# A new order table for a hand-scheduled attention and feed-forward kernel: the operations behind the first 86 in another order, and some of them on other engines

## Chip, cores and metric

One Trainium2 chip, one of its NeuronCores. The metric is the device time of the program in microseconds, the median of several runs; smaller is better. A profile is one further execution, taken by the hardware profiler, with its own time.

## The reference

```python
B, H, S, D = 4, 8, 768, 64           # batch, heads, sequence, head size
scores = q @ k.transpose(0, 1, 3, 2) / sqrt(D)
keep = (pos_k < 4) | ((pos_q - pos_k >= 0) & (pos_q - pos_k < 128))
a = softmax(where(keep, scores, -1e9))
x = (a @ v).transpose(0, 2, 1, 3).reshape(B * S, H * D)      # 3072 x 512
h = maximum(x @ w_in, 0)                                      # w_in 512 x 2048
out = (h * h) @ w_out                                         # w_out 2048 x 512
```

Attention with 4 sink keys and a window of 128 keys, then a two-layer network with a squared ReLU. All inputs and the output are float32; inside, the matmuls run on bfloat16.

## The kernel before

**Tiles.** The four batches are worked through one after the other, each batch in three blocks of 256 query rows (s = 0, 1, 2). A block's attention handles head pairs; pairs 0 and 1, and 2 and 3, are taken together. TensorE makes transposed scores of a head pair in a PSUM bank `ps` (L614, function `scores`); ScalarE takes the exponential into the SBUF tile `expm` (L635, `expo`); the window's triangles are cut out either by a multiplication with `tri` on VectorE (L647) or by two selects on GpSimd (L219, `domask`); TensorE multiplies with the values into `po` (L683, `values`); VectorE divides by the sums into `xn_sb` (L699, L700, `norm`). Sink keys and values go through a small product `pk` (L573) and `es`. The result has to be transposed for the network: batches 0 and 1 do it on TensorE (`px`, L732, "bridge") with a copy to `xT`; batches 2 and 3 do it by DMA transposes from SyncE's queue (L714).

**Loads.** In batch 0 and 1, q and k are cast by DMAs that GpSimd issues (L373) and transposed on TensorE (`pt`, L508), then copied to `qkT` ("unload", by VectorE or ScalarE). In batches 2 and 3, GpSimd issues the casting loads of q, k and v (L404, L416), and SyncE issues DMA transposes into `qkT` (L462). w_in and w_out come by four loads each, also from GpSimd (L317 for w_out).

**Network.** Batch 0's first layer is done plainly (L764), that of the others in a form with seven products per quad and sums of inputs and weights (L892; sums `xs`, `wi`). The second layer of two row blocks is seven products (L1239) with sums `sg` and `wt`; a quarter of the result is copied out of PSUM to the buffer `osb` and others are added to it (L1253). The store of a pair of row blocks is one DMA from SyncE (L1282). `osb` has two buffers, so a third pair waits for the first one's store to land.

**Order.** 996 operations are created by the code above; each has a number (in order of creation), the engines that it may run on, and the buffers that it takes. The table `ORDER` is a string of these numbers. `Plan.run` goes through it and records each operation's instructions; so the table sets the order of instructions on every engine and every queue. A letter behind a number (p, d, a, g) chooses the engine (TensorE, VectorE, ScalarE, GpSimd); without it the first of its list is taken. `+0` or `+1` chooses the PSUM pool. Engines run their own instructions in that order, and wait by semaphores for what they need. DMAs stand in the instruction order of the engine that issues them, so one that must wait holds up what is behind it on that engine.

**Numbers used below.** 156, 162, 168, 174: first layer of batch 0, block 0 (L764). 81: its sink scores. 106, 108, 116, 118: masks of batch 0, block 1, for head pairs 0, 1, 2, 3. 109, 111, 119, 121: the values of these pairs. 123, 125: the block's two bridge transposes; 31, 32: the last V loads of batch 0; 33 to 36: the loads of w_out; 208: sink values of batch 1; 129: an unload of batch 0, block 2; 137: the scores that read it; 172: a relu. 466 to 477: the DMA transposes of batch 2's q and k; 692 to 709: the loads of batch 3. 296, 315, 334: the three stores of batch 0; 548, 586, 567: the stores of batch 1. 553, 556: first and second product of a chain of the second layer; 555: the copy between them into `osb`.

Of the kernel before, what the change touches and what calls it, by code (L numbers as in the profile page):

```python
# [20 lines left out]
ORDER = """  # L21
994 0 1 2 7 8 9 10 11 12 13 14 15 16 17 18 995+0 3 5 19 20 21 6 79 22 23 24 25 55d 56d 57+0 58 59 60a 83+0 85 103+1
105 26 27 28 62d 61d 63+1 64 67d 68d 65a 69+0 70 71 72 66a 84+1 73a 74a 75+1 76 78 91+0 86 77a 93 80 113+1 87+0 92+1
89 94 95+0 97 115 88 90 96 98 114+1 99+0 101 117 100 104+0 102 4 29 106 30 107 81+1 31 82 156+0 109+1 116 118 162+0
108d 32 111 157 112 119+1 168+0 121 120 110 123+1 122 125 174+1 163 126 335 169 124a 171+0 131+0 128+1 33 208 34 164
133 170a 175 35 36 37 172 38 132 39 40 158 130a 129a 144+1 146 137+0 176 136+0 147d 145+1 138 140 139d 177+0 278 134+0
148 159+1 135 149d 141d 142+0 279 143 173a 41 178 150+1 282+0 42 151 179a 152+0 43 153a 280 160 154 44 165+0 155a 45
274 189+1 166 180+1 275 276 284 161a 127 285 190d 277 281 283 181 337 286 287 46 192+1 289 196+0 193 200+0 194 197
167a 47 195a 201 297 336 288 48 202 338 183+0 198a 199a 203a 212+0+0 49 290 182 292 184d 215 294 230+0+1 291 299 50
293 298 191 213 231 186+1 204+0 233 295 185 187d 51 52 300 206a 301+0 251+1 303 248+0 205 188a 207a 232d 249a 304 253  # L30
252a 339 316 305d 296 302 219+1+0 216 317 308 53 318 209 306 307d 220 54 222 214 210+0 250a 319 309 234 448 237+0+1
310 311 211 235+0 238 217+0 240 218 236 223 340 466 239d 320+0 449 312 241d 221 450 322 256+0+0 451 259 257 313 452
453 323 454 455 314 341 321 456 242+0 244+0 457 324 458 224+1 327 459 325 460 461 243 471 225 326 226+0 254+1 246 245a
329 228 330 229a 247a 227 331 315 347+1 343 363+1 342 349 469 345 328 332 365 348 364 344 346 255 351 350 333 367
263+1+1 462 366 353 369d 352 479 354 260d 264 368 370 355d 379+0 470 467 266 358 356 468 395+0 258 359 463 371 372
357a 374 360d 361 381 265 373a 380 376 267d 375 474 383 261+0 382 362a 377 397 396 268+0 477 384 262 385 399 386 270+0
475 398 269 387d 272 273 378a 400 473 401 464 478 465 402 271a 489+0+0 390 411 492 490 388 392 403d 391 334 406 404
407 482+0+0 412 393 432+0 483 433 389 476 434 416+1 472 413 394 408 409 436 414 405 417 418 435 534+0 410a 438 420 692
419 536 437 530 422 439 415 421 693 423 532 440 537 485 443 441 491 424 694 427 533 538 444 695 442a 429 696 697 493
531 445 425 539 494+0 428 446 426a 535 495 480+0 540 430 698 447a 498+1+0 481 699 484 486 544 700 499 543 487+0 549  # L40
501 431 488 568 545 713 572+0 505+0+0 569 574 500d 546 541 508 506 542 573 521+0+0 547 710 714 701 579 522 570 575 576
514+1+0 509d 571 496 702 577 703 524 715 578 507 510+0 548 515 523d 582 580 550 723 497 581 583 502 517 585 553+0 551
503+0 511 704 711 516 554 584 587 588 592+0 589 504 594 525 526+0 705 590 518d 555 527 593 717 556 557 591 519+0 712
716 596 520 558 559d 598 552 749+0+0 706 707 595 722 560 561 563 512 750 752 597 599 513 600 562 742+0+0 753d 565d 528
564 603 743 601 751 602 566 604 745 586 726+0+0 529 720 605d 721 608+0 727 609 606 610 660+1 661 662 611 729 624 644+0
718 663 626 612 730 719 724+0 613 625 567 614 725 615 754+0 616 607 728 664 665 645 617 666 646 755 667 618a 648 647
668 619 744 620 649 627 650d 651 731+0 746 669 621 671 672 708 622 676+0 670a 677 673 732 652 674 747+0 623 678 655
653 679 680 656 681 675a 748 657 658 628+1 629 682 630 659 733+1+0 683 774 632 631 734 778+0 684 654a 775 634 685 735
633 779 635 686a 780 636 776 687 688 736 777 709 756 781 689d 690 758+0+1 759 637 782 761 639 640 638a 737 738+0 783
641d 739 642 691a 785 765+0+0 762d 784 760 643 797+0 768 766 793 787 757 799 794 788 769 789 763+0 795 740 767d 790d  # L50
741 791 764 798 786 831 800 801 836+1 837 834 802 832 792 838d 852+0 833 854d 853 840 804 796 855 856 803 839 806 858d
770+0 771 807 857 812 835 813 859 842 808 841 843 772 805 814 810 816+1 860 773 863 861 817 865 844d 864 847 845 809
823 866 818d 846a 868 848 867a 872+0 869 849 874 871 920+0 862 819 850 820 922 873 904+1 870 815 921 905 875 906d 876
877 923 851a 924 821 936 822d 878 879 907 925 811 926 908 880 825 883 827 937 927 881 826 938 882 828 910 885 824 829
884 909 886 888+1 911 928d 889 887 940+0 890 892 942 891 929 893 939 931 894d 932 912 915 930a 895 933 896 934 943 913
916 897 899 914a 944 900 945 935 917 830 946 901 898 941 959+0 902 918 949 947 919a 903 955 957 950 951 956 953 948
961 960 974 962 966 952d 976 978+1 963 975 958 979 964 981+1 965d 954 980 968 967 977 982 983d 970 969 985 984 986 989
972 987 971 988 990 973 993 992 991
"""
DUMMIES = {  # L60
    995: 29, 58: 8, 63: 10, 64: 4, 83: 3, 91: 3, 97: 3,
# [1345 lines left out]
```

## Time and profile before

| | |
|---|---|
| time, median of 3 runs | 210.18 us (210.08 to 210.21) |
| profiled execution, own time | 209.92 us |
| its span, first to last instruction | 208.1 us |
| TensorE busy | 198.7 us, 95% |
| VectorE, ScalarE, GpSimd busy | 175.4, 140.0, 94.0 us |
| granted TensorE clock | 1.000 |

Engines are named PE (TensorE matmuls), PEld (its weight loads), DVE (VectorE), ACT (ScalarE), POOL (GpSimd) and SP (SyncE); a q behind the name is the engine's queue, which issues DMAs. A row of a timeline reads: start, length, engine and line, operation, what it writes from what it reads, count; in brackets the idle time before it and who ended it. A row of waits reads: who waited for whom, total, times, longest. The ends of matmuls are modelled, and successive matmuls overlap, so a row of sixteen ends later than the next one begins.

### The profile page before, as it was taken

What the parts mean: (1) busy time and instruction counts of PE and PEld (TensorE: products, weight loads), DVE (VectorE), ACT (ScalarE), POOL (GpSimd) and SP (SyncE); (2) the same over time, 40 slices, a digit from 0 to 9 for tenths busy, and PEclk for the clock granted to TensorE, in tenths of its full rate; (3) what the DMA queues carried; (4) which work ended last, traced back from release to release, by engine and by line L of the source; (5) the groups of instructions that cost most, each with busy time, mean ns of one, the idle gap of its engine ahead of it and who ended that gap; (6) DMA issues with size and microseconds to landing.
All of it is one profiled execution on the core that took longest, in us unless ns stands there. A gap on an engine that the chain in (4) does not pass through costs nothing.

```text
span 208.1 us, 6073 instructions
## 1 busy us (share of the span) xinstructions
PE 198.7 (95%) x2524; PEld 178.7 (86%) x2524; DVE 175.4 (84%) x343; ACT 140.0 (67%) x218; POOL 94.0 (45%) x134
## 2 busy tenths in 40 slices
PE   7779989999999999999999999999999999999993
PEld 7548878998888889889878989998889999999892
DVE  5844647988998899999997988999999998999753
ACT  2686679865895579999977459789892176475010
POOL 7999983597289907319629937100230000000000
PEclk9999999999999999999999999999999999999999
DMA  5999999999999999999999998902022230110205
GB/s 169 278 187 206 174 197 215 166 150 142 158 68 146 147 198 154 166 142 82 143 133 214 110 149 161 186 3 50 3 50 104 30 126 3 41 60 3 101 3 202
DMA packets 93995, 26.12 MB, mean 125 GB/s; under 512 B 86800, under 2 KB 91408, under 8 KB 93968
## 3 DMA queue, kind: packets, MB, share of 16 engines
q0 software_dynamic: 69248, 12.59, 87.1%
q1 hardware_dynamic: 24536, 13.01, 28.7%
q8 instruction: 20, 0.33, 0.6%
q10 hardware_dynamic: 184, 0.14, 0.2%
q14 instruction: 7, 0.06, 0.1%
HBM read 27.30 MB, written 6.29 MB: 161 GB/s over the span
## 4 chain that ended last, share of the span: by engine, by line
PE 70%; DMA 13%; POOL 5%; ACT 4%; DVE 3%; SPq 2%; issue 1%; ACTq 0%; DVEq 0%; POOLq 0%
PE py L1239 31%; PE pm L892 23%; DMA w_out_sb<-in_moe_w_out_dram 6%; PE po L683 5%; PE ps L614 5%; DMA qn<-in_q_dram 4%; DMA qr<-in_q_dram 3%; PE pm L764 2%; POOL expm L219 2%; PE py L1100 2%; SPq L352 2%; ACT expm L635 1%; PE pt L508 1%; ACT gT_sb L915 1%; POOL qn L373 1%
## 5 line engine op out<-in xcount | busy, mean ns | idle before, releaser
L635 ACT ACTIVATE expm<-ps 128x1024 bf16<-128x1024 f32 (+1 forms) x48 | 43.8, 956 | 4.3 <-PE ps L614 3.9
L219 POOL TENSOR_SCALAR_AFFINE_SELECT expm<-expm 128x512 bf16<-128x512 bf16 x30 | 20.9, 726 | 42.2 <-ACT expm L635 33.6
L942 DVE CUSTOM_DVE_ANT_0 r<-pm,t 128x512 bf16<-128x512 f32 x54 | 36.1, 684 | 2.3 <-ACT t L193 1.4
L1239 PEld LDWEIGHTS <-gT_sb 128*128 128x128 bf16 x352 | 33.0, 98 | 4.6 <-issue 1.1
L892 PEld LDWEIGHTS <-w_in_sb 128*128 128x128 bf16 x384 | 32.7, 114 | 1.0 <-issue 0.5
L193 ACT ACTIVATE t<-pm 128x512 f32<-128x512 f32 x42 | 24.9, 599 | 12.3 <-PE pm L892 11.1
L193 ACT ACTIVATE osb<-py 128x256 f32<-128x256 f32 x36 | 13.6, 384 | 26.1 <-PE py L1239 23.7
L1239 PEld LDWEIGHTS <-sg 128*128 128x128 bf16 x264 | 24.9, 98 | 3.4 <-issue 0.8
L892 PEld LDWEIGHTS <-wi 128*128 128x128 bf16 x288 | 24.8, 114 | 0.8 <-issue 0.5
L1239 PE MATMUL py<-wt,sg 128*128 128x256 bf16 x176 | 22.8, 273 | 0.0
L1239 PE MATMUL py<-w_out_sb,gT_sb 128*128 128x256 bf16 x176 | 22.7, 273 | 0.0
L1239 PE MATMUL py<-wt,gT_sb 128*128 128x256 bf16 x176 | 22.7, 273 | 0.0
L764 PE MATMUL pm<-xT,w_in_sb 128*128 128x256 bf16 x192 | 22.5, 273 | 0.1
L915 ACT ACTIVATE gT_sb<-r 128x1024 bf16<-128x1024 bf16 x21 | 22.1, 1058 | 0.7 <-DVE r L942 0.7
L892 PE MATMUL pm<-xs,w_in_sb 128*128 128x256 bf16 (+1 forms) x192 | 21.3, 246 | 0.0
L892 PE MATMUL pm<-xs,wi 128*128 128x256 bf16 (+1 forms) x192 | 21.2, 246 | 0.0
L764 PEld LDWEIGHTS <-w_in_sb 128*128 128x128 bf16 x192 | 20.6, 114 | 0.6 <-issue 0.2
L683 PE MATMUL po<-v,expm 128*128 128x65 bf16 x352 | 18.0, 193 | 0.4 <-ACT expm L635 0.3
L700 DVE TENSOR_TENSOR xn_sb<-po,rc 128x512 bf16<-128x512 f32 (+1 forms) x28 | 17.2, 615 | 1.0
L683 PEld LDWEIGHTS <-expm 128*128 128x128 bf16 x352 | 16.8, 97 | 1.4 <-issue 0.6
L614 PE MATMUL ps<-qkT 64*128 64x128 bf16 (+1 forms) x256 | 14.5, 238 | 1.4 <-ACT qkT L193 1.1
L1253 DVE TENSOR_TENSOR osb<-py,osb 128x256 f32<-128x256 f32 x33 | 13.3, 418 | 2.8 <-PE py L1239 1.9
(107 smaller groups left out, 372.1 us busy)
## 6 DMA issues: line engine op xcount, KB each, us to landing
out_dram<-osb SPq DMA_DIRECT2D x11, 512.0 KB, 3.1
v<-in_v_dram POOLq DMA_DIRECT2D x24, 128.0 KB, 7.0
qn<-in_k_dram POOLq DMA_DIRECT2D x20, 128.0 KB, 6.6
qn<-in_q_dram POOLq DMA_DIRECT2D x20, 128.0 KB, 6.9
w_in_sb<-in_moe_w_in_dram POOLq DMA_DIRECT2D x4, 512.0 KB, 10.1
w_out_sb<-in_moe_w_out_dram POOLq DMA_DIRECT2D x4, 512.0 KB, 9.8
qr<-in_k_dram SPq DMA_DIRECT2D x4, 256.0 KB, 5.3
qr<-in_q_dram SPq DMA_DIRECT2D x4, 256.0 KB, 4.8
```

Source lines behind the costliest of these rows:

```text
L193: return nc.scalar.activation(out=dst, in_=src, func=AF.Copy)
L219: nc.gpsimd.affine_select(out=e_tile, in_=e_tile, compare_op=ALU.is_ge, fill=fill, base=i - 1, pattern=[[0, n], [1 if i else -1, 128]], ch ...
L614: nc.tensor.matmul(ps[:, h2, o:o + w], lhsT=qkT_sb[r, m, 1, c, :], rhs=qkT_sb[r, m, 0, qb:qb + w // 128, :], start=(i == 0 and not biased) ...
L635: nc.scalar.activation(out=x[:, :, o:512], in_=bank_t["s", b, s, m][:, :, o:512], func=AF.Exp, scale=scale)
L683: touch(("po", b, s, m0), e, nc.tensor.matmul(pv[:, i, h2, :], lhsT=lhsT, rhs=rhs, start=(n_ == 0), stop=(n_ == len(mms) - 1)), j)
L700: touch(("po", b, s, m0), e, nc.vector.tensor_tensor(out=xn_sb[:, 2 * s:2 * s + 2, 128 * (m0 + j0):128 * (m0 + j0 + nj)].rearrange("p i (j ...
L764: nc.tensor.matmul(pm[:, i, :], lhsT=w_in_sb[:, fb // 4, kb, fb % 4:512:4], rhs=xT[:, c0 // 256:(c0 + cw) // 256, kb, :], start=(kb == 0), ...
L892: touch(tag, e, nc.tensor.matmul(y[:, bk, i, :], lhsT=weights(name, f0 + i, a), rhs=rhs[:, a, :], start=fresh and i == 0 and a == 0, stop= ...
L915: nc.scalar.activation(out=d, in_=x, func=AF.Square)
L942: touch(tag, e, nc.vector._custom_dve(TENSOR_ADD_SAT, out=d.rearrange("p n c -> p (n c)"), in0=T["y"][:, 1].rearrange("p n c -> p (n c)"), ...
L1239: touch((b, u), e, nc.tensor.matmul(region(name), lhsT=x[:, i, :], rhs=w_[:, i, :], start=first and i == 0, stop=i == HB - 1, skip_group_c ...
L1253: ins = nc.vector.tensor_tensor(out=d, in0=region(of), in1=d, op=ALU.add)
```

## The change

The string `ORDER` is replaced. The first 86 words stay; behind them the same operations stand in another order, some with another engine letter or another PSUM pool. Nothing else in the file differs.

In all, 31 operations go from ScalarE to VectorE, 22 from VectorE to ScalarE, 6 masks from VectorE to GpSimd, and 6 masks and one building of sink values from GpSimd to VectorE. The order of the DMAs changes too: on SyncE, the third store of batch 0 (334) goes from behind ten of the twelve DMA transposes of batch 2 to behind three of them, and the first store of batch 1 (548) from behind five of the next transposes to behind seven.

The diff, cut:

```diff
@@ -21,41 +21,41 @@
 105 26 27 28 62d 61d 63+1 64 67d 68d 65a 69+0 70 71 72 66a 84+1 73a 74a 75+1 76 78 91+0 86 77a 93 80 113+1 87+0 92+1
-89 94 95+0 97 115 88 90 96 98 114+1 99+0 101 117 100 104+0 102 4 29 106 30 107 81+1 31 82 156+0 109+1 116 118 162+0
-108d 32 111 157 112 119+1 168+0 121 120 110 123+1 122 125 174+1 163 126 335 169 124a 171+0 131+0 128+1 33 208 34 164
-133 170a 175 35 36 37 172 38 132 39 40 158 130a 129a 144+1 146 137+0 176 136+0 147d 145+1 138 140 139d 177+0 278 134+0
...
-310 311 211 235+0 238 217+0 240 218 236 223 340 466 239d 320+0 449 312 241d 221 450 322 256+0+0 451 259 257 313 452
...
+89 94 95+0 97 115 88 90 96 98 114+1 99+0 101 117 100 104+0 102 4 29 106 156+1 30 81+0 157d 107 116 118 82 31 162+1
+119+1 109+0 163 110 120 108 158a 121 32 127 33 111 34 168+0 35 112 123+1 122 125 169 164a 174+1 126 124 208d 171+0 36
+131+1 170a 175 335 133 128+0 172 129 132 176 278 37 144+1 280 38 137+0 130a 136+0 146 177+0 39 140 145+1 40 41 42 43
...
+345 347+1 254+1 331 344 255 349 363+1 466 456 348 333 457 351 458 350 365 364 332 328 367 334 469 470 353 459 263+1+1
...
+716 575 524 715 576 525d 514+1+0 515 702 509 522 548 523 577 714 571 579 578 581 587 703 580 553+0 502d 550 582 704
+584 555 583 510+0 588 517 556 503+0 585 705 511 589 706 518d 554 557d 526+0 591 504 712 592+0 516 717 519+0 558 594
...
```

More of the change, by code (lines that the diff above doesn't have):

```diff
@@ L23 @@
 105 26 27 28 62d 61d 63+1 64 67d 68d 65a 69+0 70 71 72 66a 84+1 73a 74a 75+1 76 78 91+0 86 77a 93 80 113+1 87+0 92+1
-89 94 95+0 97 115 88 90 96 98 114+1 99+0 101 117 100 104+0 102 4 29 106 30 107 81+1 31 82 156+0 109+1 116 118 162+0
-108d 32 111 157 112 119+1 168+0 121 120 110 123+1 122 125 174+1 163 126 335 169 124a 171+0 131+0 128+1 33 208 34 164
-133 170a 175 35 36 37 172 38 132 39 40 158 130a 129a 144+1 146 137+0 176 136+0 147d 145+1 138 140 139d 177+0 278 134+0
-148 159+1 135 149d 141d 142+0 279 143 173a 41 178 150+1 282+0 42 151 179a 152+0 43 153a 280 160 154 44 165+0 155a 45
@@ L28 @@
[L28 to L31, printed above, removed]
-310 311 211 235+0 238 217+0 240 218 236 223 340 466 239d 320+0 449 312 241d 221 450 322 256+0+0 451 259 257 313 452
@@ L33 @@
[L33 to L57, printed above, removed]
@@ L58 @@
-972 987 971 988 990 973 993 992 991
+89 94 95+0 97 115 88 90 96 98 114+1 99+0 101 117 100 104+0 102 4 29 106 156+1 30 81+0 157d 107 116 118 82 31 162+1
+119+1 109+0 163 110 120 108 158a 121 32 127 33 111 34 168+0 35 112 123+1 122 125 169 164a 174+1 126 124 208d 171+0 36
+131+1 170a 175 335 133 128+0 172 129 132 176 278 37 144+1 280 38 137+0 130a 136+0 146 177+0 39 140 145+1 40 41 42 43
+44 45 147d 138 134+0 139d 159+1 141d 148 337 135 178 142+1 149d 150+0 143 160 151 282+0 152+0 173a 284d 46 336 153 154
@@ new lines @@
+274 279 275 276 179a 165+1 281 155a 161 166 180+1 47 167a 338 189+0 48 283 277 196+0 285 289 181 190 200+0 286d 49 339
+192+1 287 50 288 193 290 51 202a 197 201 195a 198a 297 194 203a 292 52 183+0 191a 199 299 212+0+0 291 213 294d 184d
+293 295 215 230+0+1 204+1 186+1 231 205 182 233 298 53 301+0 248+0 216 296 185 234d 187 188 206 207a 316 303 251+0 304
+232d 250a 341 249a 305 54 219+0+1 252a 302 300 306 308 209 220 210+0 318 253 222 211 223 237+0+1 221 307 240 235+0 448
+309 311 214 238 320+0 449 217+0 450 310 236 342 467 322d 312 451 323 313 452 239d 453 218 324 256+0+0 257 314 454 317
@@ new lines @@
+224+1 325 241d 455 321 259 225 319 315 468 226+0 227a 242+1 243 340 244+0 228 326 327 245 330 229a 329 246 247a 343
+345 347+1 254+1 331 344 255 349 363+1 466 456 348 333 457 351 458 350 365 364 332 328 367 334 469 470 353 459 263+1+1
+460 366 352 258 354 346 266 368 369d 260 370 471 461 355d 264 358 356 371 462 360d 379+0 395+0 357a 381 359 380 374
+372 397d 463 361 373a 362a 375 376 396 261+0 383 377 265 398 464 465 267 399 382 474 385 268+0 262 269 384 386 378a
+270+0 272 401 476 387d 475 400 273 402 478 271a 388 489+0+0 411 403d 390 404 492 473 391 406 490 414 392 412 407
@@ new lines @@
+482+0+0 393 413 432+0 692 389 483 693 434 433 416+1 436 417 472 408 418 405 477 409 493 435 410a 534+0 394 419 438 420
+422 437 530 439 694 695 713 421 423 440 536 424 443 415 532 445 441 537 696 697 444 425 427 428 698 491 538 711 485
+426a 531 533 494+0 535 699 446 479 539 429 495 442a 430 540d 480+0 484 481 486 498+1+0 499 431a 501 544 447 487+0
+572+0 543 488 710 545 568 700 701 574 505+0+0 547 541 508 569 573 570 542 546d 506 549 496 551 500d 497 521+0+0 507d
+716 575 524 715 576 525d 514+1+0 515 702 509 522 548 523 577 714 571 579 578 581 587 703 580 553+0 502d 550 582 704
@@ new lines @@
+584 555 583 510+0 588 517 556 503+0 585 705 511 589 706 518d 554 557d 526+0 591 504 712 592+0 516 717 519+0 558 594
+593 520 527 596 590 749+0+0 595 512 598 559d 552 752 513 560 750 597 562 599 742+0+0 753d 743 563 600d 745 561 564
+751d 603 565 726+0+0 727 528 601 722 529 566 602 604 608+0 609 660+1 723 605d 707 720 661 610 606 721 624 718 611 662
+729 612 719 613 663 614 724+0 725 607 644+0 730 615 625 744 626 754+0 728 755 746 616 664 619 666 645 665 617 646 627
+667 618a 567 620 668 647 648 731+0 621d 669 671 649 672 650 622 651 670a 676+0 673 732 652 678 674 623 675a 747+0 677
@@ new lines @@
+655 628+1 653 748 680 679 657 656 629 630 682 681 658 733+1+0 774 734 683 775 776 684 685 632 659 778+0 779 736 687
+686a 586 631 688 689d 634 690 654a 633 635 758+0+1 780d 781 735 636 759 756 639 637 782 737 738+0 641d 761 739 640 740
+741 642 638a 777 783 784 785 691a 643 793 765+0+0 787 794 795 788 768 766 708 762d 797+0 789 790d 799 798 760 709 786
+831 804 800 832 757 791 836+1 763+0 812 852+0 801 838 833 796 837 834 802 767 764 769d 853 792 805 854 856 855 839 840
+842 858 835 803d 857 770+0 813 841 771 843 807 844d 806 859 847 845 860 816+1 863 848 808 861 814 809d 772 864 818
@@ new lines @@
+849d 850 773 810 851a 819 820d 904+1 865 868 866 920+0 846a 867a 821 872+0 874 869 870 873 815 811 862 822d 936 921
+817 922 823 876 875 825 923 878 877 938 826 824 879 828d 827 880d 871 924 925 883 926 885 881 884 829 888+1 939 905
+906 886 890d 889 908 927 882 907 892 928d 887a 910 940+0 891 909 937 894 911 893 929 895 931 912 932 930 942 913 896
+933d 897 943 914a 941 898 934 899 944 915 830 935 916 901 917 900 945 959+0 946 950 918 902 919a 949 903 955 952 961
+974 947 957 951 958 956 978+1 948 962 963 976 953 975 977 960 964 954 966 979 965 981+0 968 969 967 980 983 984 970
@@ L59 @@
+982 985 986 989 971d 972 973 987 988 990 993 992 991
 """
```

## Prediction, made before the changed kernel ran

> **What bounds the kernel now.** I read the page first, then who TensorE waited for, then the order of time on GpSimd, TensorE and the queue of SyncE.
>
> ```profile
> span 208.1 us, 6073 instructions
> ...
> PE 198.7 (95%) x2524; PEld 178.7 (86%) x2524; DVE 175.4 (84%) x343; ACT 140.0 (67%) x218; POOL 94.0 (45%) x134
> ```
>
> TensorE is busy for 95% of the span. The change removes and adds no instruction, so TensorE's own work stays; only its waits can go or come. The first 86 operations stand as they did; on TensorE they reach to 16.8 us, so I asked for its waits from 15 us to the last matmul:
>
> ```profile
> PE ps L614 <- ACT qkT L193: 0.6, 1, 0.6
> PE px L732 <- DVE xn_sb L700: 0.4, 1, 0.4
> PE po L683 <- ACT expm L635: 0.3, 1, 0.3
> PE ps L614 <- ACT r L776: 0.3, 1, 0.3
> PE pt L508 <- DMA qn<-in_q_dram: 0.2, 1, 0.2
> PE pk L573 <- ACT expm L635: 0.2, 1, 0.2
> ```
>
> The columns are total, times and longest. The sum is 2.0 us, and the third row (at 15.07 us) belongs to operation 97, which is in the unchanged part. So 1.7 us, 0.8% of the span, is all that a better order can take from these waits. What it can lose has no such bound. The rest of this is a search for places where the new order makes TensorE wait.
>
> **The engines.** In the new order 31 operations go from ScalarE to VectorE, 22 back, 6 masks from VectorE to GpSimd and 7 operations from GpSimd to VectorE: VectorE gets 10 more, ScalarE 9 fewer, GpSimd one fewer. Ten of some 0.6 us (as the mask and copy rows below) make VectorE's 175.4 some 181 us, under TensorE's 198.7: as a sum it costs nothing, and the cover is TensorE's own work. If that cover were gone it would be these 6 us. What is left are places.
>
> **Place 1: a mask goes to GpSimd, behind a load (operation 108).** Head pair 1 of the second block of batch 0 was masked on VectorE at 18.01 us; now GpSimd does it, after the masks 116 and 118 and the issue of a V load (31).
>
> ```profile
> 17.97 0.89 POOL L373 DMA_DIRECT2D qn<-in_q_dram  x1
> 18.85 0.88 POOL L382 DMA_DIRECT2D v<-in_v_dram  x1
> 19.73 2.39 POOL L219 TENSOR_SCALAR_AFFINE_SELECT expm<-expm 128x512 bf16<-128x512 bf16 x4
> 22.07 0.89 POOL L382 DMA_DIRECT2D v<-in_v_dram  x1
> 22.96 0.56 POOL L317 DMA_DIRECT2D w_out_sb<-in_moe_w_out_dram  x1
> 23.53 1.80 POOL L555 TENSOR_TENSOR vs<-vs_in,head_rows 32x130 bf16<-32x130 f32 x4
> ```
>
> GpSimd in the new order: the q load ends at 18.86, four selects 2.39 to 21.2, V load 0.88 to 22.1, two selects more, half of 2.39, to 23.3.
>
> ```profile
> 16.77 0.29 PE L573 MATMUL pk<-qkT,kblk 128*32 128x256 bf16 x4
> 17.03 1.91 PE L764 MATMUL pm<-xT,w_in_sb 128*128 128x256 bf16 x16
> ...
> 19.14 1.91 PE L764 MATMUL pm<-xT,w_in_sb 128*128 128x256 bf16 x16
> ...
> 24.70 0.29 PE L732 MATMUL px<-ident,xn_sb 128*128 128x128 bf16 x2 [0.40 <-DVE xn_sb L700]
> ```
>
> TensorE in the new order runs first layer 156, sink scores 81, first layer 162, then the values 119, 109, 121 and 111, which needs mask 108. From 17.03 to 19.14 lie now one layer group and one value group; a layer group is 16 matmuls at 0.109, 1.75 (its 1.91 counts the tail of the last matmul, under which the next begins), which leaves 0.36 for the values. So 1.75 for 156, 0.29, 1.75 and three times 0.36 reach 111 at 21.9. It waits until 23.3: **+1.4 us**. Queued behind it are first layer 168, both transposes of the bridge, and with them ScalarE's relus. Lower end: entering and leaving the sink scores may take 0.2 more of TensorE's time, which shortens the wait to 1.2. Upper end with slow selects, whose shortest, median and longest stand here:
>
> ```profile
> L219 POOL TENSOR_SCALAR_AFFINE_SELECT expm<-expm x30: 624/636/1084, 16.8 to 154.2; 128x512 bf16<-128x512 bf16 x30
> ```
>
> two at 1084 ns take 2.2 in place of 1.2, so 2.4 us. I take the middle one, because VectorE does only the normalising of these values then (xn_sb from po and rc), as when the rows at 19.73 ran at 0.60 each. The Trainium skill, page "SBUF — State Buffer", section "SBUF: two separate sides", says that VectorE and GpSimd share a port pair under an exclusive lock, taken by a VectorE operation with two inputs in SBUF; by that rule the slow selects would be those that met VectorE's masks, and the wait here would be 2.4 only if one of those fell beside it; none does in the new order.
>
> **What goes.** The same order puts the last two bridge transposes after 168 and the normalising well before: the 0.4 at 24.70 goes. The unload 129 that S137 waits for leaves ScalarE's queue (behind relu 172 and unload 130) for VectorE: of the 0.6 (ScalarE's row) some 0.2 stays, as a copy must still follow its transpose. The 0.2 for the q load at 48 us is a landing time; arriving 0.3 later or more, TensorE does not meet it. Together **-1.0 us**. The 0.3 for relu 172 and the 0.2 before the sink scores keep their producers: nothing.
>
> Sink values of batch 1 move from GpSimd (1.80, row at 23.53) to VectorE, where no row shows them; between 0.4 (four of the shortest, about a tenth each) and 1.80, ahead of copies that TensorE wants only at 28 us, after 1.75 us of first layer: nothing at either end. The w_out loads are issued later: the first after mask 108 and a V load, 24.2 at the earliest and not 22.96, with the building of mask constants also ahead. Transfers queue, as their median from issue to landing shows, so the price lies between nothing and the 1.2 of the issue, and TensorE itself comes later by then: I take nothing and keep +0.5 for the range.
>
> ```profile
> w_out_sb<-in_moe_w_out_dram POOLq DMA_DIRECT2D x4, 512.0 KB, 9.8
> ```
>
> One group of scores stands alone that stood beside another; 0.1 by the gaps of 16.77 to 17.03.
>
> **Place 2: stores change their place in SyncE's queue.** The third store of batch 0 now stands ahead of nine transposes of batch 2; before, it stood ahead of two. It waits for its last sum:
>
> ```profile
> 76.84 0.41 DVE L1253 TENSOR_TENSOR osb<-py,osb 128x256 f32<-128x256 f32 x1
> ```
>
> ```profile
> 72.44 12.10 SPq L462 DMA_TRANSPOSE qkT<-qn  x8
> 84.64 1.30 SPq L1282 DMA_DIRECT2D out_dram<-osb  x1
> ```
>
> ```profile
> 86.04 2.98 SPq L462 DMA_TRANSPOSE qkT<-qn  x2
> ```
>
> The transposes' own durations, and their times to landing (shortest, median, longest):
>
> ```profile
> L462 SPq DMA_TRANSPOSE qkT<-qn x24: 1188/1220/2400, 61.3 to 130.1; - x24
> ...
> DMA to landing us min/median/max: 2.5/4.7/8.7
> ```
>
> So SyncE stands until 77.3, where it ran eight transposes from 72.44. Store 1.30 and nine transposes of 1.22 (their median) to 1.51 (12.10/8) end at 89.6 to 92.2; before, the last ended at 89.0. Batch 3's loads into the same buffers follow these transposes:
>
> ```profile
> 93.66 1.75 POOL L404 DMA_DIRECT2D qn<-in_q_dram  x2 [4.33 <-DMA qkT<-qn]
> ...
> 98.85 1.80 POOL L404 DMA_DIRECT2D qn<-in_q_dram  x2
> ```
>
> They start 0.6 to 3.2 later than 93.66, and the q load issued at 98.85 at 99.4 to 102.0; it took this long to land:
>
> ```profile
> qn<-in_q_dram POOLq DMA_DIRECT2D x1, 128.0 KB, 7.5
> ```
>
> that is 106.9 to 109.5. SyncE now holds a transpose that needs it, one more transpose, and only then batch 1's first store. Two transposes of 1.25 with their gaps put the store at 109.5 to 112.1. Its output buffer is wanted again: ScalarE's first copy of the next pair of row blocks (operation 555) waits for the store to land. The stores' times to landing:
>
> ```profile
> DMA to landing us min/median/max: 2.6/3.1/6.9
> ```
>
> With 3.1 it lands at 112.6 to 115.2; with the transposes' 4.7 around it, up to 116.8.
>
> ```profile
> 112.36 2.62 PE py L1239 x24
> ...
> 118.20 0.87 PE py L1239 x8
> ```
>
> These are pieces of the chain of waits. Up to 114.98 the same products run in both orders; then the new order wants product 556, which stood at 118.20 before, and 556 needs that copy, 384 ns on ScalarE:
>
> ```profile
> L193 ACT ACTIVATE osb<-py 128x256 f32<-128x256 f32 x36 | 13.6, 384 | 26.1 <-PE py L1239 23.7
> ```
>
> So the store must land by 114.6, plus the 0.4 by which TensorE is late from place 1. The difference runs from 2.4 early to 1.8 late. I take **+0.5 us** and keep 0 and 2.2 (1.8 and the copy's queue) as ends. Behind the waiting copy stand ScalarE's exponentials; VectorE and TensorE wait for them, so a late landing is paid once.
>
> **The sum.** 1.4 - 1.0 + 0.1 + 0.5 = +1.0 on the profiled execution, whose own time is 209.92 us (span 208.1 and 1.8 around it): 210.9. The median of the runs, 210.18, is 0.26 above that execution; with it **211.2 us**.
>
> **Rivals.**
> - The store lands in time: +0.5 alone, 210.7. For it: the store's shortest landing of 2.6 and issue-bound transposes. Against it: loads and transposes share the engines just there.
> - The store is late in full: +2.2 in place of 0.5, 212.9; with w_out's 0.5, 213.4. It is decided by when batch 3's q loads can start.
> - Faster: place 1's wait is taken in by later waits. TensorE's own later waits are for work at fixed times (a landing at 48 us, ScalarE's queue); every one that it arrives at late is shortened. If all the 1.7 goes and place 1 costs 1.2, the result is 0.5 lower, 209.7; it decides from the point where the four value groups before 111 cover more than 1.2 of the mask, and place 2 must cost nothing. The small waits hidden under modelled matmul tails speak for it: the gap at 24.70 is wider than its 0.40.
> - The order makes no difference: loss and gain within 0.4 of each other, 210.2. It needs about 0.6 more gain than I find.
>
> **Chances and range.** A measurement of this kernel tells about 0.2% (0.4 us) from no change. Forecast 0.35; store in time 0.20 (just over that bound, half of it in same); store late in full 0.15; faster 0.20; no difference 0.10. Slower 0.35 + 0.10 + 0.15 = 0.60, same 0.10 + 0.10 less a little, 0.17, faster 0.23. The likeliest case alone spans 210.8 to 211.8; to hold 8 in 10 the range reaches from 209.6 to 212.9.
>
> **What would show it.** Right: a wait of TensorE for GpSimd's expm before L683 near 22 us of 1 us or more, no idle at the bridge two microseconds later; SyncE idle before L1282 from about 71 to 77 us; batch 3's q loads issued after 94 us; a wait of L1239 for ScalarE's osb near 115 us. Wrong: no wait at 22 us (then mask 108 was not on the path), a store landed before 114 us, or a new wait in the last 80 us, where I found no change that matters.

## The result, and the profile after

The new order took 211.66 us in the median of 22 runs (210.29 to 214.20), the order before 210.27 beside it (22 runs, 209.42 to 213.41). The ratio is 1.0052 with a 95% interval of 1.0028 to 1.0076, slower by about 1.1 us. Like every ratio below, it leaves out the slow runs, those more than 1.5% above the fastest of the same kernel: six of the 22 here, one of the 22 before. The 22 times of the new order lie in two groups, twelve from 210.29 to 211.78 and ten from 212.72 to 214.20, so the median says less than usual; the profiled execution took 210.80 and stands in the lower group. Nine of the ten upper ones had a mean granted clock of 0.996 or more, so a lower clock does not make that group.

The page's first lines of the new order:

```profile
span 209.1 us, 6063 instructions
...
PE 200.1 (96%) x2524; PEld 179.4 (86%) x2524; DVE 179.6 (86%) x356; ACT 138.8 (66%) x209; POOL 90.8 (43%) x130
```

VectorE has 4.2 us more and stays under TensorE. Whom TensorE waited for, from 15 us on (total, times, longest):

```profile
PE po L683 <- POOL expm L219: 0.9, 2, 0.6
PE pm L764 <- DMA w_in_sb<-in_moe_w_in_dram: 0.3, 1, 0.3
PE po L683 <- ACT expm L635: 0.3, 1, 0.3
PE ps L614 <- ACT r L776: 0.3, 1, 0.3
PE py L1239 <- DVE osb L1253: 0.2, 1, 0.2
```

The waits for the bridge, for the unload and for the q load are gone, and one for GpSimd's masks has come. Its place, in the order of time on TensorE and on GpSimd:

```profile
19.16 2.39 POOL L219 TENSOR_SCALAR_AFFINE_SELECT expm<-expm 128x512 bf16<-128x512 bf16 x4
21.50 0.89 POOL L382 DMA_DIRECT2D v<-in_v_dram  x1
22.40 1.23 POOL L219 TENSOR_SCALAR_AFFINE_SELECT expm<-expm 128x512 bf16<-128x512 bf16 x2
```

```profile
22.28 0.23 PE L683 MATMUL po<-v,expm 128*128 128x65 bf16 x2
22.34 0.19 PE L683 MATMUL po<-vs,es 128*128 128x65 bf16 x1
23.10 0.20 PE L683 MATMUL po<-v,expm 128*128 128x65 bf16 x1 [0.57 <-POOL expm L219]
23.68 0.20 PE L683 MATMUL po<-v,expm 128*128 128x65 bf16 x1 [0.38 <-POOL expm L219]
```

The four selects are masks 116 and 118, then comes the V load, then mask 108 in two selects. In brackets is the idle time behind the modelled end of the last matmul; by their starts the value groups follow each other at 0.03, so 22.34 to 23.10 costs 0.73 and 23.10 to 23.68 another 0.55: 1.28 us, not 0.95.

SyncE's queue, at the third store of batch 0 and at the first of batch 1:

```profile
68.36 2.77 SPq L462 DMA_TRANSPOSE qkT<-qn  x2
77.91 0.34 SPq L1282 DMA_DIRECT2D out_dram<-osb  x1
78.34 23.90 SPq L462 DMA_TRANSPOSE qkT<-qn  x12
105.13 3.37 SPq L714 DMA_TRANSPOSE xT<-xn_sb  x2
108.60 2.52 SPq L462 DMA_TRANSPOSE qkT<-qn  x2
111.21 0.53 SPq L1282 DMA_DIRECT2D out_dram<-osb  x1
```

and the same store of batch 1 in the order before:

```profile
107.74 0.53 SPq L1282 DMA_DIRECT2D out_dram<-osb  x1
```

SyncE stands from 71.1 to 77.9, as forecast; the store of batch 1 is issued at 111.21 (107.74 before), behind four transposes. The loads of batch 3 on GpSimd and ScalarE's copy 555:

```profile
93.23 1.75 POOL L404 DMA_DIRECT2D qn<-in_q_dram  x2 [0.69 <-DMA qkT<-qn]
...
98.42 1.80 POOL L404 DMA_DIRECT2D qn<-in_q_dram  x2
```

```profile
115.06 0.38 ACT L193 ACTIVATE osb<-py 128x256 f32<-128x256 f32 x1 [0.77 <-DMA out_dram<-osb]
```

The q loads start 0.4 earlier than before, not later, and the store lands at 114.98; the copy waits 0.77 for it, TensorE only 0.19 by its starts.

To see where the time goes over the whole kernel, the starts of the same operations on TensorE are compared wherever both orders have done the same work. The difference in us, after less before, changes mainly here:

| stretch | new order | new order, profiled again |
|---|---|---|
| at 12 us, before the first changed word | +0.24 | -0.13 |
| to the bridge transpose 123: mask 108, weights of 162 | +1.73 | +1.80 |
| bridge 125 no longer waits | -0.58 | -0.57 |
| scores 137 no longer wait for unload 129 | -0.74 | -0.74 |
| the q load at 48 us is met late enough | -0.35 | -0.35 |
| the rest of the kernel, in steps under 0.35 | +0.37 | +0.22 |
| at the last common point | +0.67 | +0.23 |

So one place costs 1.7 us and three places give 1.7 back. What is left in these two executions, from 12 us to the last common point, is +0.43 and +0.36. From there to the end of the span they take another 0.29 and 0.36 more (4.92 and 4.99 us against 4.63); three executions of versions of the order before take 4.73 to 4.94 there, so this last part is not shown to come from the order.

### The profile page after: what moved, and what is told of

It reads as the page before. It is cut to its first block, busy times and chain, and to the rows that moved or that the text cites. A ratio compares the mean times of both kernels' runs of the same rounds, so it can differ in the third digit from the quotient of the medians.

```text
span 209.1 us, 6063 instructions
## 1 busy us (share of the span) xinstructions
PE 200.1 (96%) x2524; PEld 179.4 (86%) x2524; DVE 179.6 (86%) x356; ACT 138.8 (66%) x209; POOL 90.8 (43%) x130
## 4 chain that ended last, share of the span: by engine, by line
PE 75%; DVE 9%; ACT 5%; DMA 3%; POOL 3%; SPq 2%; issue 1%; ACTq 0%; DVEq 0%
PE py L1239 30%; PE pm L892 21%; PE pm L764 9%; PE po L683 5%; PE ps L614 5%; DMA qr<-in_q_dram 3%; ACT expm L635 3%; POOL expm L219 2%; PE py L1100 2%; DVE r L942 2%; SPq L352 2%; PE pt L508 2%; DVE xn_sb L700 1%; DVE sg L1213 1%; DVE t L195 1%
## 5 line engine op out<-in xcount | busy, mean ns | idle before, releaser
L942 DVE CUSTOM_DVE_ANT_0 r<-pm,t 128x512 bf16<-128x512 f32 x54 | 36.6, 686 | 1.5 <-PE pm L892 0.6
L193 ACT ACTIVATE t<-pm 128x512 f32<-128x512 f32 x44 | 25.7, 598 | 18.1 <-PE pm L892 17.0
L1239 PEld LDWEIGHTS <-gT_sb 128*128 128x128 bf16 x352 | 33.6, 98 | 4.6 <-issue 0.8
L193 ACT ACTIVATE osb<-py 128x256 f32<-128x256 f32 x29 | 11.0, 385 | 15.2 <-PE py L1239 12.6
L404 POOL DMA_DIRECT2D qn<-in_k_dram x12 | 10.9, 926 | 11.6 <-PE pt L508 7.4
```

Of the source, the lines that this page charges most:

```text
L193: return nc.scalar.activation(out=dst, in_=src, func=AF.Copy)
L404: return [nc.gpsimd.dma_start(out=qn_t[b, ti][:, t, :].rearrange("p (h d) -> p h d", d=D), in_=(q, k)[ti][b, :, 128 * t:128 * t + 128, :]. ...
L942: touch(tag, e, nc.vector._custom_dve(TENSOR_ADD_SAT, out=d.rearrange("p n c -> p (n c)"), in0=T["y"][:, 1].rearrange("p n c -> p (n c)"), ...
L1239: touch((b, u), e, nc.tensor.matmul(region(name), lhsT=x[:, i, :], rhs=w_[:, i, :], start=first and i == 0, stop=i == HB - 1, skip_group_c ...
```

## The experiments

All versions move words of the order table, nothing else. Theory A: the loss is the mask (place 1) and the store (place 2), each at its length. Theory B: the landings of transposes and loads decide, and what one place gives up is waited for at the next.

**Each edit undone alone, in the new order.** The `...` marks words left out. The mask back on VectorE, right behind mask 118:

```diff
-... 116 118 82 31 162+1 119+1 109+0 163 110 120 108 158a ...
+... 116 118 108d 82 31 162+1 119+1 109+0 163 110 120 158a ...
```

> The changed order with one operation put back: mask 108 on VectorE, right behind ScalarE's exponential 107, as before the change. My theory (the mask on GpSimd costs TensorE 1.3 us near 23 us, and a store that lands late costs some executions 2 us more near 115 us): TensorE's wait for GpSimd's expm at L683 goes; 0.3 to 0.6 of it comes back as the waits at the bridge and for the q load at 48 us, so the quick executions fall from about 210.7 to 209.7-210.1, and the slow group near 213 stays, about 1 us lower. Rival (the mask is the whole loss, and the spread of the changed kernel's times is noise of the chip): all executions at or under 210.2. Rival (the mask's wait is cover for other work, as in the prediction's faster case): no change of more than 0.3.

Median 211.62 (209.36 to 213.71, 12 runs), ratio to before 1.0007 (0.9965 to 1.0049). The fastest execution is 0.9 below the new order's fastest (210.29), and the upper group stays, as expected. The median is the new order's, but the order before was at 210.81 beside it, on another chip, so the ratio is the fairer number: lower than 1.0052, with intervals that overlap. What the mask gives is lost again in some executions. The profiled one took 213.71; its waits:

```profile
PE ps L614 <- DMA qkT<-qn: 1.4, 1, 1.4
PE py L1239 <- ACT osb L193: 1.0, 2, 0.9
PE pm L764 <- DMA w_in_sb<-in_moe_w_in_dram: 0.6, 1, 0.6
```

GpSimd's row is gone. The second row is the store's: product 556 waits for copy 555. The first is one that the prediction had not named: at 122.55 us the scores 749 wait for a transpose of k and q of batch 3 (714 or 717), which stand behind the store in the queue; 717 landed at 124.16.

The third store of batch 0 back behind transpose 473:

```diff
-... 367 334 469 470 353 ...  492 473 391 ...
+... 367 469 470 353 ...  492 473 334 391 ...
```

> The changed order with the third store of batch 0 (334) put back behind the transpose 473, where it stood before. My theory: SyncE no longer idles from about 71 to 77 us, batch 3's q loads start some 1 to 3 us earlier, the first store of batch 1 lands before ScalarE's copy 555 wants the buffer, and the group of executions near 213 is gone; the quick group stays at 210.3 to 211. Rival (the spread has another cause): two groups as before, 210.3-211.8 and 212.7-214.2.

Median 215.09 (213.01 to 216.63, 6 runs), ratio 1.0195 (1.0136 to 1.0255): the expectation fell, the edit costs some 3 us by the ratios. The profiled execution (213.01, the fastest) shows where the early store helps; these are GpSimd's loads of batch 3:

```profile
90.06 1.83 POOL L404 DMA_DIRECT2D qn<-in_k_dram  x2 [3.30 <-DMA qkT<-qn]
96.59 1.76 POOL L404 DMA_DIRECT2D qn<-in_q_dram  x2 [4.70 <-DMA qkT<-qn]
```

With the store ahead of them, the last two transposes of batch 2 (472, 477) are issued at 89.13 and 90.73, on either side of the first k load at 90.06, and take 3.2 and 5.2 us to land (477 at 95.88). In the new order both are issued ahead of the k loads (at 90.73) and land in 2.5, the last at 92.59. The q loads, which wait for them, start at 96.59 in place of 93.23. This execution is 2.2 above the new order's profiled one, in waits that are each 0.8 or less in its rows; what the slower executions met is not known.

The first store of batch 1 ahead of transposes 716 and 715:

```diff
-... 716 575 524 715 576 525d 514+1+0 515 702 509 522 548 523 ...
+... 548 716 575 524 715 576 525d 514+1+0 515 702 509 522 523 ...
```

> The changed order with batch 1's first store (548) moved in SyncE's queue ahead of the transposes 716 and 715, which wait for loads. My theory: the late thing is this store, held up behind those two; it is issued about 108 us and lands before 112, and the group near 213 goes although the loads start as late as in the changed order. Rival (what is late in the slow executions is a transpose or a load that TensorE or ScalarE needs itself): the group near 213 stays.

Median 211.06 (210.48 to 212.50, 12 runs), ratio 1.0035 (1.0005 to 1.0065), and no execution above 212.5: the group near 213 is gone, as expected. The store is issued at 108.52 and lands at 111.97; the wait for osb is gone from the profiled execution, which is the slowest of the twelve:

```profile
PE ps L614 <- DMA qkT<-qn: 1.6, 1, 1.6
PE po L683 <- POOL expm L219: 1.0, 2, 0.7
```

Again the scores 749 wait, at 121.2 us, until transpose 717 lands at 122.95; it was issued at 115.43, in the new order at 114.64. Place 2 thus has two ends, the store and the transposes behind it in one queue: moving the store forward moved the transposes back.

All three edits together:

> All three edits together. My theory: the sum, one group at 209.6 to 210.1, 0.1 to 0.6 us under the kernel before. Rival (each wait removed is met again further on): 210.2 or more.

Median 212.94 (209.32 to 214.15, 12 runs), with two executions at 209.32 and 210.09 and ten from 211.76 up; the ratio of 1.0021 (0.9968 to 1.0074) rests on the lowest five. The expectation fell, and its rival, that a removed wait is met again further on, fits. The third store behind 473 brings its late q loads with it (97.75 us). In the profiled execution, the slowest, ScalarE then waits until 115.45 for transpose 497 (landed at 115.34), and copy 555, behind it in ScalarE's queue, starts at 116.67:

```profile
PE py L1239 <- ACT osb L193: 3.1, 2, 3.0
```

**Mask and store, without the third store.** Both edits of the first and the third version:

> The new order with two edits at once: mask 108 on VectorE right behind mask 118, and store 548 ahead of transposes 716 and 715. Theory A, the two places are the whole loss: both waits go, so about 1.2 below the run with the store alone (211.06): median 209.7 to 210.1, no wait of L683 for POOL, none of L1239 for osb above 0.3. Theory B, the landings decide: what the mask gives up, TensorE only spends earlier at the scores 749, which wait for the transposes 714 and 717 at a fixed time: median 210.6 to 211.3, and a wait of L614 for DMA qkT of 1.5 or more near 122 us.

Median 210.97 (209.12 to 213.68, 12 runs), ratio 0.9983 (0.9953 to 1.0013). The profiled execution (211.34) has one wait of TensorE above 0.3:

```profile
PE ps L614 <- DMA qkT<-qn: 1.3, 1, 1.3
```

This is Theory B's median and its place, with a wait slightly under the 1.5 that it named: without the mask's wait TensorE reaches the scores 749 at 120.33, and transpose 717 lands at 121.83; in the new order's profiled execution they start at 121.77, behind a landing at 120.90. Yet four of the twelve executions are under 210.0, as Theory A has it, and what TensorE met in those is not known.

**The same with SyncE's order of before at 98 to 118 us.**

```diff
-713 711 710 496 497 716 715 548 714 712 717
+713 710 714 496 715 548 497 711 717 712 716
```

(the places of these words in the table stay; only which of them stands where changes) and mask 108 on VectorE:

> The new order with mask 108 on VectorE right behind mask 118, and on SyncE the order of before for the transposes and the store of 98 to 118 us (713 710 714 496 715 548 497 711 717 712 716). Theory A (mask and store are all): the same as the run with mask and store alone, 209.7 to 210.1. Theory B (landings of 714 and 717 decide): 0.7 to 1.5 below that run, 209.3 to 209.9, and no wait of L614 for DMA qkT above 0.5; if both theories are wrong, 211 or more with a wait elsewhere.

Median 210.63 (209.29 to 211.95, 12 runs) beside 210.83 of before; ratio 1.0011 (0.9983 to 1.0039). The profiled execution, the fastest, has no wait for a landing but that of w_in:

```profile
PE pm L764 <- DMA w_in_sb<-in_moe_w_in_dram: 0.6, 1, 0.6
PE po L683 <- ACT expm L635: 0.3, 1, 0.3
PE ps L614 <- ACT r L776: 0.3, 1, 0.3
PE py L1239 <- ACT osb L193: 0.2, 1, 0.2
```

The store lands at 109.91, transposes 714 and 717 at 106.36 and 113.17, all well ahead of their readers. So the wait that Theory B named is gone with its cause. The number of neither theory came: Theory B's 0.7 to 1.5 below the version before (210.97) is 0.3 in the median, and the ratio did not fall at all (0.9983, then 1.0011), so no gain is shown. What did change is the slowest execution, 211.95 in place of 213.68.

The same order on SyncE alone, with mask 108 left on GpSimd behind the V load:

> The new order with SyncE's order of before for the transposes and the store of 98 to 118 us, and mask 108 left on GpSimd behind the V load: place 1 alone. Theory A (a wait early in the kernel costs what it lasts): 1.0 to 1.4 above the run that had the mask on VectorE as well (210.63), so 211.6 to 212.0, with the wait of L683 for POOL near 22 us at 1.2 to 1.4 and none of L1239 or L614 for a landing. Theory B (later waits are for landings at fixed times and take it in): within 0.4 of 210.63.

Median 211.89 (210.45 to 213.26, 12 runs), ratio 1.0044 (1.0013 to 1.0074); the wait for GpSimd is 0.89 and 0.55 by the starts, none for a landing above 0.5. That is the number of Theory A, though the 210.63 was measured on another chip. On the same chip as this one ran the version with the mask on VectorE and one more edit, the values 109 ahead of the first layer 162:

```diff
-... 118 108d 82 31 162+1 119+1 109+0 163 ...
+... 118 108d 82 31 109+0 162+1 119+1 163 ...
```

> The version with mask 108 on VectorE and SyncE's order of before, and the values 109 ahead of the first layer 162, which waited 0.6 to 0.85 us for its weights: 109 takes 0.36 and its mask 106 is done at 17.9 us, so 0.3 to 0.4 of that wait is filled: 0.3 below that version, median 210.2 to 210.5, wait of L764 for w_in_sb 0.2 to 0.5. Rival: the values then wait for something else there (their PSUM bank or the V load), no gain.

Median 210.78 (209.60 to 212.23, 12 runs), ratio 0.9993 (0.9960 to 1.0026). The 0.3 expected of the added edit did not come: the values themselves waited 0.52 there, as its rival said. As a partner it puts the mask at 1.1 us (211.89 to 210.78), but the two intervals touch, and the new order itself, with its mask on GpSimd, had a median of 210.67 on this chip (last run below). So medians do not settle the mask's price. The fastest executions point to about 1 us, the mask being what differs between the rows:

| mask 108 on | fastest execution of each version, us |
|---|---|
| GpSimd | 210.29 and 210.16 (new order, twice), 210.48 (store early), 210.45 (order of SyncE), 213.01 (third store back) |
| VectorE | 209.36, 209.32, 209.12, 209.29, 209.60 |

The 213.01 stands apart by its third store. Of versions measured on one chip, the mask on GpSimd is 1.1 above on one (210.48 against 209.36) and 0.6 to 0.9 on another (210.16 and 210.45 against 209.60).

**The parts alone, in the order before.** The third store ahead of nine transposes:

```diff
-... 333 367 263+1+1 ...  391 334 406 ...
+... 333 367 334 263+1+1 ...  391 406 ...
```

> The order before with one edit: the third store of batch 0 (334) ahead of nine transposes of batch 2, as in the new order. The prediction's step: SyncE idle about 5 us before that store, the transposes end 0.6 to 3.2 later, so do the first loads of batch 3 behind them (94.3 to 96.9 us in place of 93.7); no wait of TensorE from it, since the products 556 stand late here: within 0.4 of before. Rival: transposes that run later find the loads done and land sooner, so the loads of batch 3 start no later than 93.7, and the time is the same or lower.

Median 210.94 (210.13 to 211.87, 10 runs), ratio 1.0023 (0.9996 to 1.0049): no difference that this can tell. SyncE's and GpSimd's rows:

```profile
72.83 2.12 SPq L462 DMA_TRANSPOSE qkT<-qn  x1
77.64 0.33 SPq L1282 DMA_DIRECT2D out_dram<-osb  x1
78.06 12.56 SPq L462 DMA_TRANSPOSE qkT<-qn  x9
```

```profile
94.77 1.75 POOL L404 DMA_DIRECT2D qn<-in_q_dram  x2 [3.85 <-DMA qkT<-qn]
```

Here the q loads are 1.1 later (94.77 against 93.66), within the prediction's 0.6 to 3.2: the step holds with the order of transposes that stood before, and not with the new one.

The mask on GpSimd, behind masks 116 and 118 and a V load:

```diff
-108d 32 111 157 ...
+32 108 111 157 ...
```

> The order before with one edit: mask 108 on GpSimd instead of VectorE, behind masks 116 and 118 and one V load, as in the new order. Theory A: the values 111 wait for GpSimd by 1.2 to 2 us near 22 us, of which the bridge's 0.4 and the 0.6 at 30 us are absorbed or not: median 0.8 to 1.6 over the runs of before beside it. Theory B (later waits are for landings at fixed times, so that this is paid in part twice or not at all): within 0.5 of before.

Median 215.32 (212.84 to 216.37, 6 runs), ratio 1.0207 (1.0158 to 1.0256): 4.5 us, far over both theories. The profiled execution was the fastest, 212.84, and its new wait is 2.57 and 0.55 by the starts. It is longer than in the new order because the values 111 stand right behind the first layer 162 here. That explains 3 us, not 4.5, so the kernel ran once more:

> The order before with mask 108 on GpSimd once more (median 215.32 over six runs, of which its profile, 212.84, was the lowest and showed no other new wait than 2.8 us for the mask). Theory A (an early wait costs what it lasts): this execution is again near 212.8, and the 215s were disturbed runs: then nothing new is in the profile. Theory B (a shift of 3 us early changes what the transposes and loads meet later): the profile is near 215 and shows besides the mask's wait one for a landing, DMA qkT or osb, of 1.5 to 3 us between 85 and 130 us.

Median 215.73 (215.44 to 216.12, 4 runs), ratio 1.0244 (1.0212 to 1.0275). The profiled execution took 215.81. Its longest wait for a landing is 0.4, at 135 us, so Theory B, which named 1.5 to 3, falls for this gap; and 212.8 did not come again, so Theory A as it was put falls too. In order of time, TensorE's first layer 168 in the two executions of this one kernel, first that of 212.84, then that of 215.81:

```profile
24.59 1.91 PE L764 MATMUL pm<-xT,w_in_sb 128*128 128x256 bf16 x16
26.34 0.23 PE L683 MATMUL po<-v,expm 128*128 128x65 bf16 x2
```

```profile
25.64 3.42 PE L764 MATMUL pm<-xT,w_in_sb 128*128 128x256 bf16 x16
28.91 0.22 PE L683 MATMUL po<-v,expm 128*128 128x65 bf16 x2
```

The same 16 matmuls take 1.75 from start to start of what follows, and then 3.27. The granted clock has the reason. The trace lists it by stretches, and in all fourteen profiled executions the stretches up to the last are whole multiples of 3.41 us, counted from a first entry at 4 to 7 us (4.86 in the execution of 215.81, 5.59 in that of 212.84). So busy time is counted in windows of 3.41 us on that grid; in each row come the window, its length, busy time of PE, PEld, DVE, ACT and POOL with their instructions, then the granted clock, the DMA share and GB/s. First the execution of 215.81:

```profile
21.93:25.34 3.41, 0.74 (x19) 0.64 (x20) 0.00 (x0) 0.78 (x1) 3.38 (x7) 1.00 1.88 177
25.34:28.75 3.41, 3.41 (x26) 2.55 (x23) 1.63 (x6) 0.00 (x0) 3.22 (x8) 0.50 2.42 165
```

TensorE was granted half its clock for one window, right behind the window that holds most of the long wait. In the execution of 212.84 a boundary, at 22.65, cuts the wait in two, and the clock stays at 1.00:

```profile
19.24:22.65 3.41, 1.66 (x16) 1.39 (x13) 0.00 (x0) 1.34 (x2) 3.40 (x7) 1.00 1.35 205
22.65:26.06 3.41, 2.37 (x38) 2.27 (x39) 1.53 (x6) 0.00 (x0) 3.20 (x7) 1.00 2.36 153
```

The wait was 2.57 and 0.55 there, 2.73 and 0.55 here. That the wait brings the half clock is read from its place in the window, not tried by itself. The other executions of this kernel agree with it: the nine of 215.19 to 216.37 have a mean granted clock of 0.988 to 0.992, the one of 212.84 has 0.998. By the starts the clock costs 1.5 us of the gap of 3.0; the rest lies in the start (0.55 at 12 us), the weights of 162 and this wait (0.35 together), 0.1 in the slowing values, and some 0.4 at the sink scores at 135 us.

**The new order once more**, beside the versions with the mask alone and with the values ahead:

> The new order once more, unchanged, beside the others: median 211.2 to 212.2. Theory A+B together (mask, store and late transposes) says that its times fall in two groups, 210.3 to 211.5 and 212.5 to 214, and that an execution of the upper one shows a wait of L1239 for ACT osb or of L614 for DMA qkT of 1 us or more between 114 and 124 us, which one of the lower has not. If an execution above 212.5 shows neither, the theory of the two groups falls.

Median 210.67 (210.16 to 214.41, 12 runs) beside 210.82 of before, ratio 1.0000 (0.9977 to 1.0024): below the 211.2 that was expected at least, and no slower than before. On this chip ten of twelve executions stand between 210.16 and 210.92, and the profiled one (210.41) has neither of the two late waits, as expected of that group. The other two, 212.50 and 214.41, were not profiled, so for the new order itself it is not shown that the upper group is made by those waits; it was seen only in versions of it.

## Why the prediction was right

The forecast of 211.2 us, slower, is close to the 211.66 measured, and the sign holds in the interval of the first measurement. In the repeat beside other versions the rival "no difference" would have been right (ratio 1.0000), so that the sign came is in part luck. By its steps:

- **Bound, and that no engine sum matters: right.** TensorE went to 96%; VectorE's 179.6 is near the 181 that was worked out.
- **Place 1, +1.4: right in mechanism and size.** 1.28 by the starts in the profiled execution, 1.41 in the second. The queue on GpSimd ran as written down: four selects in 2.39, the V load in 0.89, two selects in 1.23. The page "SBUF — State Buffer" of the Trainium skill, section "SBUF: two separate sides", whose rule spoke for slow selects only beside a VectorE operation with two inputs in SBUF, agrees with the traces on both sides: here none ran beside them, and in the version with mask 108 on VectorE and SyncE's order of before (a mask of 0.78 at 19.72) the four selects took 2.86. The prediction read the rule too narrowly, as masks alone: of the seven selects over 0.7 us in the order before, three (963 to 1084 ns) had no mask beside them but products or sums of SBUF tiles.

```profile
18.71 2.86 POOL L219 TENSOR_SCALAR_AFFINE_SELECT expm<-expm 128x512 bf16<-128x512 bf16 x4
```

- **Not seen: the weights of 162.** With the sink scores and the first layers moved together, TensorE meets the load of w_in at 18.90 and waits until 19.51, 0.59. As mask 108 ends at a fixed time, this only shortened the wait at 111; with the mask away it stays (0.37 to 0.9 in the profiled versions without the values ahead), which is one reason why the mask is worth about 1 us and not the whole 1.7.
- **What goes, -1.0: right in its three places, too small.** -0.58, -0.74 and -0.35 make -1.67. What failed is the price: the rows of waits (0.4, 0.6, 0.2) count idle time behind the modelled end of a matmul, and the starts had gaps of 0.56, 0.77 and 0.34 already before the change. Moreover nothing stayed of the unload's wait, where 0.2 was left. The rival "faster" had named this; with place 1 at 1.28 and the weights of 162 in front of it, that gain was used up.
- **Sink values on VectorE, w_out later: nothing, right.** No wait for either in the rows.
- **Place 2, +0.5: the store's time right by a wrong way, its price smaller.** The store was issued at 111.21 (109.5 to 112.1 forecast) and landed at 114.98 (112.6 to 115.2), against 115.0 as the time by which it must land. TensorE paid 0.19 for it, and nothing in the second profiled execution (landing at 114.45): inside the bounds of 0 and 2.2, under the 0.5 taken. But the link in between fails: batch 3's q loads did not come later (93.23, not 94.3 or more), because the last transposes of batch 2, issued ahead of the k loads, landed in 2.5 us. The store is late for a plainer reason: 716 and 497 stand ahead of it, and these two took 3.4 us of issue. With the transposes in the order before, the loads do come 1.1 later, as the version with the third store alone shows.
- **The late store, and what it spares.** The rival of a store late in full saw its price (up to 2.2) and not that transposes 714 and 717 stand behind the store in the same queue: the scores 749 wait 1.3 to 1.6 for those in the profiled executions of three versions. The prediction has no term for that wait.
- **The sum.** 1.4 - 1.0 + 0.1 + 0.5 = 1.0 was forecast; 0.43 and 0.36 stand in the two profiled executions up to the last common point, 0.71 in both with the end. The rest is in executions of the upper group, ten of 22 in one measurement and two of twelve in the other. So the time was met, but with a smaller steady loss than forecast and a scattered one that the sum did not hold; that the two came to the forecast is luck.

No version was shown to beat the order before: the lowest ratios, 0.9983 (mask and early store) and 0.9993 (values ahead), hold 1 in their intervals, and so does the 1.0011 of the version with the mask on VectorE and SyncE's order of before, whose fastest execution is 209.29 against 209.47 on the same chip. What makes the upper group of the new order itself stays open.

## What to carry to other kernels

Price a wait of TensorE by the starts of its matmuls, not by the idle time behind modelled ends: for the three waits that went, idle time showed 1.2 us and the starts 1.67, which is what came back. A queue of transfers has no free place: what is moved forward moves something back, so ask of every transfer in the queue, not just of the moved one, when its reader comes. Where a time scatters by more than the effect, compare fastest executions and places in the trace besides medians, and repeat on another chip before a half per cent is believed.

## What the hardware showed that was not expected

- **A wait of some 3 us can cost more than its length.** With 2.73 and 0.55 us of waiting, nearly all of it in one window of 3.41 us, the granted clock was 0.50 for the next window, and 16 matmuls took 3.27 in place of 1.75; with 2.57 and 0.55 on both sides of a boundary it stayed at 1.00. It came again in the version with all three edits, where the wait of 3.0 for osb ends at 117.1:

```profile
114.97:118.38 3.41, 1.28 (x21) 1.14 (x21) 1.81 (x6) 2.51 (x4) 3.22 (x7) 1.00 2.15 131
118.38:121.79 3.41, 3.41 (x46) 2.91 (x42) 1.99 (x5) 0.00 (x0) 0.99 (x2) 0.50 2.00 162
```

  The Trainium skill, page "TensorE: Matmul & The Clock Gate", section "Part 1: The HAM clock gate (the "warmup" mystery)", says that the clock is halved after an idle window of about 3.4 us and that the window runs freely, so that its phase decides. The traces agree in the half clock, in its length and in that one kernel met it in one execution and not in another. They add that the window need not be empty: over the fourteen profiled executions, each window with up to 1.43 us of busy TensorE was followed by the half clock, the last ones of the kernel included, and none with 1.66 us or more was. The emptiest window around the new order's wait for the mask has 2.57 us of busy TensorE and 2.34 in the second profile, far from that. A mean clock of 0.992 or less is about one such window (1.7 us lost of 209, an estimate from these rows). Three of the new order's 22 executions (211.01, 211.03 and 213.47 us) had 0.990 to 0.992, and so had nine of the 94 executions of the order before that ran beside the versions, so it is not a trait of the new order. None of these was profiled, so in which stretch it fell stays open; the 0.997 of the new order's profile lies in the last 1.2 us of its span, behind the last matmul.
- **A transpose of one form lands in 2.5 or in 8 us.** 472 and 477 took 2.5 us in the new order, issued ahead of the next loads, and 477 took 5.2 where a load had been issued 0.7 us ahead of it. 717 took 3.0 to 3.2 in the versions of the new order with SyncE's order of before, issued ahead of four loads of batch 3, and 5.8 to 8.1 in the new order and its other versions, issued behind the first of them. In these places the order of a transpose against the loads of another queue goes with the time to land; other causes were not held apart.
